# Projection sessions of three halves at block borders, and expert 0's scaling on ScalarE: a mixture of experts behind a cross attention

## The chip, the cores and the metric

The kernel runs on one core of a Trainium2 chip. The metric is the time of one execution on the device, in microseconds. A core has TensorE (in the profile PE for its matmuls and PEld for its weight loads), VectorE (DVE), ScalarE (ACT), GpSimd (POOL) and SyncE (SP), each with a queue of its own that it works through in order, and they wait for each other by semaphores. TensorE writes into PSUM, which has eight banks of 128 x 512 numbers of 32 bits; ScalarE and VectorE carry its results from there to SBUF.

## The reference

`x` is (8, 8, 512, 64): batch, head, token, channel. `state` is (8, 8, 32, 64). Both parts of the attention read each other, and the joined result goes through eight experts, all of which see every row:

```python
    a = softmax(scale * x @ state.T);   xread = a @ state
    a2 = softmax(scale * state @ x.T);  sread = a2 @ x
    attn = np.concatenate([xread, sread], axis=2)        # per batch: 512 + 32 rows
    x = attn.transpose(0, 2, 1, 3).reshape(4352, 512)
    P = sinkhorn(exp(x @ w_gate))                        # 4352 x 8, 8 rounds
    for e in range(8):
        h = np.maximum(x @ w1[e], 0.0)                   # 512 -> 1024
        out += P[:, e:e + 1] * (h @ w2[e])               # 1024 -> 512
```

## The kernel before, in words

**Stages.** Up to about 137 us the kernel computes the attention, the gate with its Sinkhorn rounds, and expert 0, in an order that a small planner (`issue`, line 48) works out from estimated costs. From there on the order is written out by hand (the loop at line 872), and the change lies in that part: experts 1 to 7.

**Blocks.** The rows are cut into nine blocks (line 122). Blocks 0 to 7 hold the 512 token rows of one batch each, block 8 the 256 state rows of all batches. The loop goes through `work`, the pairs (expert e, block bi) with e from 1 to 7: 63 pairs, of which the last has a tail of its own (`layer2_last`, line 258), so that 62 go through `layer2`.

**Projection.** `xread` is a weighted sum of 32 state vectors per head, so the kernel doesn't form it for blocks 0 to 7. It multiplies the state with `w1` first: V (line 196), which `project` (line 192) makes for one pair (e, bi). V has F = 1024 columns, made in two **halves** f of 512 columns. A half is eight matmuls on tiles of 64 x 32 of the array (line 204) into two PSUM banks `v_ps`, q = 0 and 1, and two copies by ScalarE to SBUF (line 208). What I call a **session** is one uninterrupted run of such matmuls; here it is one call of `project` with two halves, four banks. Three V tiles are there at a time (line 158).

**Layer 1.** `layer1` (line 227) is a generator. Each of its eight steps makes one **hidden tile**: two matmuls of 512 columns (line 219; four of 256 columns in block 8) into a bank `hps`, and a relu by ScalarE into `Hm` (line 239). `hps` and `v_ps` share a ring of four banks, tag "h". After the fourth and the eighth step VectorE makes four sums and differences of the hidden tiles (lines 245 to 248), which I call a group of sums.

**Layer 2.** `layer2` (line 279) multiplies with seven products instead of eight, by the sums of hidden tiles and of weights (T, lines 171 to 179). It is a generator of seven steps, each one product of eight matmuls (four in block 8; line 293) and what follows it:

```python
        product(A, h(0, 0), w2h[:, :NJ, :DH], True)
        nc.scalar.copy(out=Bb[:, :nk], in_=A[:, :nk])      # line 320
        product(Eb, s(0), T[:, 0], True);  add(Eb, 1, 1)   # E
        product(Bb, s(1), T[:, 1]);        add(Bb, 0, 1)   # B
        product(A, h(1, 0), w2h[:, NJ:, :DH]); add(A, 0, 0)
        product(Bb, h(0, 1), T[:, 2]);     add(Bb, 1, 1)   # B
        product(Eb, s(2), w2h[:, NJ:, DH:]); add(Eb, 0, 1) # E
        product(Bb, h(1, 1), T[:, 3]);     add(Bb, 1, 0)   # B
```

A and E have one PSUM bank each; B has two, the `seeds` (line 318), used in turn (line 319). The profile calls the B banks Bseed. `add` (line 303) multiplies a product by the column of P for this expert and adds it to `acc` in SBUF, one VectorE instruction per 128 rows and 256 columns (line 307). So seven products sit in four banks, and a product may only go on in its bank once the add before it has read it.

**How they are woven.** Block i's layer 2 and block i + 1's layer 1 alternate by the pattern at line 885: behind the seven products stand 0, 0, 1, 2, 2, 2 and 1 hidden tiles. Behind the first product, A, stands the session for block i + 2 (line 883). Block 6 of each expert has no session, since block i + 2 is block 8, and block 7 of expert 7 has none, since nothing is left to project. A step counter (`step`, line 862) calls the loader of the next expert's weights (`load_w`, line 160) at every sixth step: four DMAs on GpSimd's queue, and later eight differences of weights on VectorE.

**Scaling.** Expert 0's result is stored in `acc` unscaled, since P isn't known yet. In expert 1 `weigh` (line 251) multiplies each block's rows in `acc` by column 0 of P, on GpSimd, one instruction per 128 rows: blocks 0 and 1 at the start of block 0, then always one block ahead (line 310).

Of the kernel before, what the change touches and what calls it, by code (L numbers as in the profile page):

```python
# [9 lines left out]
FP32 = mybir.dt.float32  # L10
FP16 = mybir.dt.float16
AX_X = mybir.AxisListType.X
ALU = mybir.AluOpType
AF = mybir.ActivationFunctionType
EPS = 1e-9


class Ring:
# [71 lines left out]
def kernel(  # L90
# [9 lines left out]
    nc = tc.nc  # L100

    B, H, S, D = x.shape
    Ns = state.shape[2]
    Dm, E = moe_w_gate.shape
    F = moe_w1.shape[2]
# [4 lines left out]
    NTB = N // 128  # L110
    NSC = S // 128
    NP = H // 2
    NQ = NP // 2
# [8 lines left out]
    blocks = [(b * S, S) for b in range(B)] + [(NX, B * Ns)]  # L122
# [10 lines left out]
    def bank(shape, dtype, name, tag="bank"):  # L133
        return pools[tag].tile(shape, dtype, name=name, tag=tag)
# [23 lines left out]
    vpool = ctx.enter_context(tc.tile_pool(name="vpool", bufs=3))  # L158
# [24 lines left out]
    w16 = [None] * E  # L183
# [5 lines left out]
    asb = actx.enter_context(tc.tile_pool(name="attn_sb", bufs=2))  # L189
    spl = actx.enter_context(tc.tile_pool(name="stprep", bufs=1))  # L190

    def project(e, bi):
        if bi == B:
            return
        w1h = w16[e][0]
        V = vpool.tile([128, NQ, F], FP16, name="V", tag="V")
        vt[(e, bi)] = V
        for f in range(F // 512):
            cols = ds(f * 512, 512)
            ps = [bank([128, 512], FP32, "v_ps", ring[0]) for _ in range(NQ)]  # L200
            for j in range(4):
                for q in range(NQ):
                    r = ((j ^ q) % 2) * 64
                    nc.tensor.matmul(ps[q][ds(j * Ns, Ns), :], stT[ds(r, 64), bi, q, ds((j ^ q) * Ns, Ns)],  # L204
                                     w1h[ds(r, 64), 2 * q + j // 2, cols],
                                     tile_position=(r, j * Ns))
            for q in range(NQ):
                nc.scalar.copy(out=V[:, q, cols], in_=ps[q])  # L208

    def hidden_ps(e, bi, fb, out):  # L210
        w1h = w16[e][0]
# [7 lines left out]
            nc.tensor.matmul(out, lhs, rhs, start=(k == 0), stop=(k == len(terms) - 1))  # L219

    vt = {}
    ring = ["bank"]
    hid = {}
    final = (E - 1, B)
    seeds = []

    def layer1(e, bi):

        t0, tn = blocks[bi]
        th = tn // 2  # L230
        Hm = hpool.tile([128, 2, NJ, S], FP16, name="Hm", tag="Hm")
        sm = hpool.tile([128, 3, NJ, S // 2], FP16, name="sm", tag="sm")
        hid[(e, bi)] = (Hm, sm)
        for j in range(NJ):
            for i in range(2):
                fb = i * NJ + j
                hps = bank([128, S], FP32, "hps", "h")
                hidden_ps(e, bi, fb, hps[:, :tn])
                nc.scalar.activation(out=Hm[:, i, j, :tn], in_=hps[:, :tn], func=AF.Relu)  # L239
                if j % 2 and i and (e, bi) != final:  # L240
                    jj = ds(j - 1, 2)
                    a11, a21 = Hm[:, 0, jj, :th], Hm[:, 0, jj, th:tn]
                    a12, a22 = Hm[:, 1, jj, :th], Hm[:, 1, jj, th:tn]
                    s1, s2, s4 = (sm[:, k, jj, :th] for k in range(3))
                    nc.vector.tensor_add(s1, a21, a22)  # L245
                    nc.vector.tensor_sub(a21, a11, a21)  # L246
                    nc.vector.tensor_sub(s2, s1, a11)  # L247
                    nc.vector.tensor_sub(s4, a12, s2)  # L248
                yield

    def weigh(b):
        if b < len(blocks):
            t0, tn = blocks[b]
            for k in range(t0 // 128, (t0 + tn) // 128):
                nc.gpsimd.tensor_scalar(out=acc[:, k, :], in0=acc[:, k, :], scalar1=Pmat[:, k, 0:1],  # L255
                                        scalar2=None, op0=ALU.mult)

    def layer2_last():
        e, bi = final
# [19 lines left out]
    def layer2(e, bi, n):  # L279
        t0, tn = blocks[bi]  # L280
        nk = tn // 256
        th = tn // 2
        Hm, sm = hid.pop((e, bi))
        w2h, T = w16[e][1], tsum[e]
        tb = t0 // 128
        p = Pmat[:, :, e:e + 1]
        A = bank([128, 2, DH], FP32, "A", "A")
        Eb = bank([128, 2, DH], FP32, "E", "E")

        def product(dst, lhs, rhs, first=False):  # L290
            for c in range(nk):
                for j in range(NJ):
                    nc.tensor.matmul(dst[:, c], lhs(j, c), rhs[:, j],  # L293
                                     start=first and c == 0 and j == 0, stop=(j == NJ - 1),
                                     skip_group_check=True)

        def h(i, half):
            return lambda j, c: Hm[:, i, j, ds(half * th + c * 128, 128)]

        def s(k):  # L300
            return lambda j, c: sm[:, k, j, ds(c * 128, 128)]

        def add(src, row, col):
            for c in range(nk):
                k = tb + row * nk + c
                dst = acc[:, k, ds(col * DH, DH)]
                nc.vector.scalar_tensor_tensor(out=dst, in0=src[:, c], scalar=p[:, k], in1=dst,  # L307
                                               op0=ALU.mult, op1=ALU.add)

        if e == 1:  # L310
            for b in range(2) if bi == 0 else (bi + 1,):
                weigh(b)
        product(A, h(0, 0), w2h[:, :NJ, :DH], True)
        if not n:
            for i in range(2):
                bb = pb.tile([128, 2, DH], FP32, name="Bseed%d" % i)
                nc.tensor.matmul(bb.rearrange("p c d -> p (c d)"), identh, aT[:, 0, 0], start=True, stop=True)
                seeds.append(bb)
        Bb = seeds[n % 2]
        nc.scalar.copy(out=Bb[:, :nk], in_=A[:, :nk])  # L320
        yield
        product(Eb, s(0), T[:, 0], True)
        add(Eb, 1, 1)
        yield
        product(Bb, s(1), T[:, 1])
        add(Bb, 0, 1)
        yield
        product(A, h(1, 0), w2h[:, NJ:, :DH])
        add(A, 0, 0)
        yield  # L330
        product(Bb, h(0, 1), T[:, 2])
        add(Bb, 1, 1)
# [54 lines left out]
    for g in range(2):  # L387
# [10 lines left out]
        out=wg_st, in_=moe_w_gate.rearrange("(kc p) e -> p kc e", p=128)))  # L398
# [28 lines left out]
    for g in range(4):  # L427
        ps = psum([128, 4, 128], FP16, "stT_ps")
# [13 lines left out]
    def gmul(_):  # L442
        for b in range(B):
            for j in range(4):
                for q in range(NQ):
# [6 lines left out]
                  lambda eng, q=q: copy(eng, G[:, :, q], gps[q].tile), [gm_op], uses=[gps[q]])  # L452
# [201 lines left out]
    def tile_of(tag, shape):  # L654
# [15 lines left out]
        out=Pmat, in_=logits, func=AF.Exp, bias=sm_["nm"]), [c])  # L670
# [137 lines left out]
    for bi in range(2):  # L808
# [14 lines left out]
        for j in range(NJ):  # L823
# [32 lines left out]
    for tag in ("A", "E"):  # L856
        pools[tag] = ctx.enter_context(
            tc.tile_pool(name="psum_" + tag, bufs=1, space=bass.MemoryType.PSUM))
    ring[0] = "h"
    n = 0  # L860

    def step():
# [6 lines left out]
                wload.pop(0)  # L869

    work = [(e, bi) for e in range(1, E) for bi in range(len(blocks))]
    for i, (e, bi) in enumerate(work):
        if bi == 1 and e + 1 < E:
            wload.append(load_w(e + 1))
        if (e, bi) == final:
            layer2_last()
            break
        l2 = layer2(e, bi, i)
        l1 = layer1(*work[i + 1]) if i + 1 < len(work) and work[i + 1] not in hid else iter(())
        for k in range(7):  # L880
            next(l2)
            step()
            if k == 0 and i + 2 < len(work) and work[i + 2] not in vt:
                project(*work[i + 2])
            for _ in range((0, 0, 1, 2, 2, 2, 1)[k]):
                next(l1, None)
                step()
        for part in (l1, l2):
            for _ in part:
                pass  # L890
        if bi == len(blocks) - 3:
            for _ in (x for w in wload for x in w):
                pass
            wload.clear()
# [30 lines left out]
```

## Time and profile before

| | |
|---|---|
| median of 3 executions | 766.16 us (766.08 to 768.02) |
| the profiled execution | 765.04 us |
| its span, first to last instruction | 763.3 us |
| granted TensorE clock, mean | 1.00 |
| busy TensorE, VectorE, ScalarE, GpSimd | 747.2, 626.8, 513.3, 104.5 us |

All rows of the profile are of one execution. Its time is 1.7 us above its span, which is what lies around the first and the last instruction.

How to read the rows. In the timeline a row has the start in us from the span's start, the duration of the merged group, the engine, the line of the kernel, the operation, output<-inputs with their shape, and the count; in brackets stands the idle time of the engine ahead of it and what ended it. Matmuls overlap, and their ends are modelled, so the distance between two starts says more than a duration. In the groups by line stand the count, then busy us and mean ns of one, then the idle time ahead. In the list of waits stand the engine and line that waited, what it waited for, the sum in us, how often, and the longest. "issue" is idle time for which the profile shows no releaser.

### The profile page before, as it was taken

What the parts mean: (1) busy time and instruction counts of PE and PEld (TensorE: products, weight loads), DVE (VectorE), ACT (ScalarE), POOL (GpSimd) and SP (SyncE); (2) the same over time, 40 slices, a digit from 0 to 9 for tenths busy, and PEclk for the clock granted to TensorE, in tenths of its full rate; (3) what the DMA queues carried; (4) which work ended last, traced back from release to release, by engine and by line L of the source; (5) the groups of instructions that cost most, each with busy time, mean ns of one, the idle gap of its engine ahead of it and who ended that gap; (6) DMA issues with size and microseconds to landing.
All of it is one profiled execution on the core that took longest, in us unless ns stands there. A gap on an engine that the chain in (4) does not pass through costs nothing.

```text
span 763.3 us, 16286 instructions
## 1 busy us (share of the span) xinstructions
PE 747.2 (98%) x6557; PEld 501.5 (66%) x6557; DVE 626.8 (82%) x1533; ACT 513.3 (67%) x1002; POOL 104.5 (14%) x102
## 2 busy tenths in 40 slices
PE   5999999999999999999999999999999999999997
PEld 3444445566776667766776666766677666767676
DVE  6998977888987888888897888888887888878885
ACT  5888976666667675766657665676656666576652
POOL 4433100799200000100001000000001000000000
PEclk9999999999999999999999999999999999999999
DMA  8997200060015000510006000240006000002334
GB/s 135 190 147 123 46 1 1 1 112 1 1 24 89 1 2 1 88 25 2 1 1 111 2 1 1 38 75 1 1 2 101 11 2 1 1 34 85 104 111 139
DMA packets 41595, 34.61 MB, mean 45 GB/s; under 512 B 16688, under 2 KB 33072, under 8 KB 41520
## 3 DMA queue, kind: packets, MB, share of 16 engines
q0 software_dynamic: 21248, 20.97, 17.7%
q1 hardware_dynamic: 19040, 12.08, 6.0%
q8 instruction: 51, 0.84, 0.5%
q10 hardware_dynamic: 1232, 0.52, 0.3%
q14 instruction: 24, 0.20, 0.1%
HBM read 42.48 MB, written 8.91 MB: 67 GB/s over the span
## 4 chain that ended last, share of the span: by engine, by line
PE 91%; DVE 5%; ACT 3%; DMA 1%; issue 0%
PE hps L219 27%; PE Bseed L293 20%; PE E L293 14%; PE A L293 13%; PE yps L769 7%; PE v_ps L204 4%; PE hps L734 4%; DVE acc L307 1%; DVE sm L245 1%; ACT Hm L239 1%; PE su_ps L609 1%; DMA st_st<-in_state_dram 1%; ACT V L370 1%; PE y L271 0%; PE v_ps L712 0%; ACT xT L370 0%
## 5 line engine op out<-in xcount | busy, mean ns | idle before, releaser
L239 ACT ACTIVATE Hm<-hps 128x512 f16<-128x512 f32 (+1 forms) x496 | 266.1, 572 | 188.4 <-PE hps L219 173.4
L219 PE MATMUL hps<-aT,V 128*128 128x512 f16 x880 | 234.9, 379 | 0.0
L293 PEld LDWEIGHTS <-Hm 128*128 128x128 f16 x1888 | 184.6, 98 | 68.9 <-ACT Hm L376 0.3
L307 DVE SCALAR_TENSOR_TENSOR acc<-Bseed,Pmat,acc 128x256 f32<-128x256 f32 x354 | 155.4, 478 | 56.6 <-PE Bseed L293 54.1
L293 PEld LDWEIGHTS <-sm 128*128 128x128 f16 x1416 | 133.1, 98 | 51.8 <-DVE sm L245 23.8
L293 PE MATMUL A<-w2h,Hm 128*128 128x256 f16 x944 | 123.5, 273 | 0.0
L293 PE MATMUL Bseed<-T,Hm 128*128 128x256 f16 x944 | 123.3, 273 | 0.0
L219 PEld LDWEIGHTS <-V 128*128 128x128 f16 x880 | 86.1, 98 | 45.2
L208 ACT CAST V<-v_ps 128x512 f16<-128x512 f32 x216 | 111.2, 608 | 0.0
L307 DVE SCALAR_TENSOR_TENSOR acc<-E,Pmat,acc 128x256 f32<-128x256 f32 x236 | 103.3, 477 | 4.5 <-PE E L293 0.9
L245 DVE TENSOR_TENSOR sm<-Hm 128x512 f16<-128x512 f16 (+1 forms) x122 | 51.1, 419 | 19.3 <-ACT Hm L239 18.5
L769 PE MATMUL yps<-w2h,hT 128*128 128x512 f16 x272 | 66.5, 380 | 0.0
L307 DVE SCALAR_TENSOR_TENSOR acc<-A,Pmat,acc 128x256 f32<-128x256 f32 x118 | 51.9, 479 | 15.8 <-PE A L293 15.7
L293 PE MATMUL E<-T,sm 128*128 128x256 f16 x472 | 63.7, 274 | 0.6
L293 PE MATMUL Bseed<-T,sm 128*128 128x256 f16 x472 | 61.8, 273 | 0.0
L293 PE MATMUL E<-w2h,sm 128*128 128x256 f16 x472 | 61.7, 273 | 0.0
L255 POOL TENSOR_SCALAR acc<-acc,Pmat 128x512 f32<-128x512 f32 x34 | 55.2, 1638 | 44.8 <-DVE Pmat L686 44.8
L166 POOL DMA_DIRECT2D w1h<-in_moe_w_dram x12 | 8.6, 720 | 355.2 <-PE hps L219 355.2
L248 DVE TENSOR_TENSOR sm<-Hm,sm 128x512 f16<-128x512 f16 (+1 forms) x122 | 52.5, 430 | 4.2
L246 DVE TENSOR_TENSOR Hm<-Hm 128x512 f16<-128x512 f16 (+1 forms) x122 | 51.0, 418 | 4.2
L247 DVE TENSOR_TENSOR sm<-sm,Hm 128x512 f16<-128x512 f16 (+1 forms) x122 | 49.4, 405 | 0.0
L320 ACT COPY Bseed<-A 128x512 f32<-128x512 f32 (+1 forms) x62 | 34.1, 549 | 18.7 <-PE A L293 17.2
(110 smaller groups left out, 561.6 us busy)
## 6 DMA issues: line engine op xcount, KB each, us to landing
w1h<-in_moe_w_dram POOLq DMA_DIRECT2D x16, 512.0 KB, 7.1
w2h<-in_moe_w_dram POOLq DMA_DIRECT2D x16, 512.0 KB, 7.7
out_dram<-acc SPq DMA_DIRECT2D x32, 256.0 KB, 2.8
x_nat<-in_x_dram POOLq DMA_DIRECT2D x16, 256.0 KB, 5.9
st_st<-in_state_dram SPq DMA_DIRECT2D x1, 256.0 KB, 4.5
st_st<-in_state_dram ACTq DMA_DIRECT2D x1, 256.0 KB, 4.9
out_dram<-acc SPq DMA_DIRECT2D x4, 64.0 KB, 1.7
out_dram<-acc ACTq DMA_DIRECT2D x4, 64.0 KB, 2.0
```

What stands on the lines that cost most here:

```text
L208: nc.scalar.copy(out=V[:, q, cols], in_=ps[q])
L219: nc.tensor.matmul(out, lhs, rhs, start=(k == 0), stop=(k == len(terms) - 1))
L239: nc.scalar.activation(out=Hm[:, i, j, :tn], in_=hps[:, :tn], func=AF.Relu)
L245: nc.vector.tensor_add(s1, a21, a22)
L246: nc.vector.tensor_sub(a21, a11, a21)
L247: nc.vector.tensor_sub(s2, s1, a11)
L248: nc.vector.tensor_sub(s4, a12, s2)
L255: nc.gpsimd.tensor_scalar(out=acc[:, k, :], in0=acc[:, k, :], scalar1=Pmat[:, k, 0:1], scalar2=None, op0=ALU.mult)
L293: nc.tensor.matmul(dst[:, c], lhs(j, c), rhs[:, j], start=first and c == 0 and j == 0, stop=(j == NJ - 1), skip_group_check=True)
L307: nc.vector.scalar_tensor_tensor(out=dst, in0=src[:, c], scalar=p[:, k], in1=dst, op0=ALU.mult, op1=ALU.add)
L320: nc.scalar.copy(out=Bb[:, :nk], in_=A[:, :nk])
L769: nc.tensor.matmul(yps.tile, hT[fb].tile[:, ds(tk * 128, 128)], w2h[:, fb, :], start=(fb == 0), stop=(fb == NFB - 1))
```

## The change

It has four parts, and all of it concerns experts 1 to 7.

1. `project` becomes a generator over a list of halves, which need not belong to one block. The table `SESS` says at the border of which blocks a session stands and how many halves it takes: three at blocks 7, 0, 2, 3 and 5, one at block 6, none at 1, 4 and 8. The very first, ahead of expert 1's block 0, takes two. A session now stands ahead of the block's first product. Of three halves the first uses the E bank and the B bank that this block is about to use; the other two use the four banks of the ring. Its first half is copied at once, the others after the A product.
2. The patterns of hidden tiles change: `PATV` in a block with a session, `PAT0` in one without, `PATS` in block 8, `PATN` in a block 7 without a session. All end with 0: no hidden tile stands behind the last product.
3. The first group of sums of each expert's block 0, which is made during block 8 of the expert before, is emitted one step later, behind the next product's add (`late`).
4. `weigh` takes one row block of 128 at a time. The first block's four go to VectorE, ScalarE, VectorE and GpSimd; all others to ScalarE, one behind each of the last four products of the block before, while expert 1 runs.

```diff
+SESS = {7: 3, 0: 3, 2: 3, 3: 3, 5: 3, 6: 1}
+PATV = (0, 0, 1, 3, 2, 2, 0)
+PAT0 = (0, 1, 1, 2, 2, 2, 0)
+PATS = (1, 1, 1, 1, 2, 2, 0)
+PATN = (1, 1, 1, 2, 2, 1, 0)
...
-    def project(e, bi):
...
+    def project(halves, n):
+        banks = []
+        for k, (e, bi, f) in enumerate(halves, 3 - len(halves)):
+            if (e, bi) not in vt:
+                vt[(e, bi)] = vpool.tile([128, NQ, F], FP16, name="V", tag="V")
+            w1h = w16[e][0]
             cols = ds(f * 512, 512)
-            ps = [bank([128, 512], FP32, "v_ps", ring[0]) for _ in range(NQ)]
+            if k:
+                ps = [bank([128, 512], FP32, "v_ps", "h") for _ in range(NQ)]
+            else:
+                ps = [bank([128, 512], FP32, "v_ps", "E"), seeds[n % 2].rearrange("p c d -> p (c d)")]
...
-            for q in range(NQ):
-                nc.scalar.copy(out=V[:, q, cols], in_=ps[q])
+            banks.append([(vt[(e, bi)][:, q, cols], ps[q]) for q in range(NQ)])
+        for dst, src in sum(banks[:-2], []):
+            nc.scalar.copy(out=dst, in_=src)
+        yield
+        for dst, src in sum(banks[-2:], []):
+            nc.scalar.copy(out=dst, in_=src)
+        yield
...
+                    if bi == 0 and j == 1:
+                        late.append(sums)
+                    else:
+                        sums()
...
-    def weigh(b):
...
+    def weigh(k, eng):
+        if eng == "ACT":
+            nc.scalar.mul(acc[:, k, :], acc[:, k, :], Pmat[:, k, 0:1])
+        else:
+            (nc.vector if eng == "DVE" else nc.gpsimd).tensor_scalar(
+                out=acc[:, k, :], in0=acc[:, k, :], scalar1=Pmat[:, k, 0:1], scalar2=None, op0=ALU.mult)
...
-        if e == 1:
-            for b in range(2) if bi == 0 else (bi + 1,):
-                weigh(b)
+        if not n:
+            for k, eng in enumerate(("DVE", "ACT", "DVE", "POOL")):
+                weigh(k, eng)
...
+    halves = [(e, bi, f) for e, bi in work if bi < B and (e, bi) not in vt for f in range(F // 512)]
     for i, (e, bi) in enumerate(work):
...
+        v, pat = iter(()), PATS if bi == B else PATN if bi == B - 1 else PAT0
+        if bi in SESS and halves:
+            some = SESS[bi] if i else F // 512
+            v, pat = project(halves[:some], i), PATV
+            del halves[:some]
+        next(v, None)
         l2 = layer2(e, bi, i)
...
         for k in range(7):
             next(l2)
             step()
-            if k == 0 and i + 2 < len(work) and work[i + 2] not in vt:
-                project(*work[i + 2])
-            for _ in range((0, 0, 1, 2, 2, 2, 1)[k]):
+            if k == 0:
+                next(v, None)
+            if late:
+                late.pop()()
+            if e == 1 and bi < B and 3 <= k < 7:
+                m = blocks[bi + 1][0] // 128 + k - 3
+                if m < NTB:
+                    weigh(m, "ACT")
+            for _ in range(pat[k]):
                 next(l1, None)
                 step()
```

More of the change, by code (lines that the diff above doesn't have):

```diff
@@ L190 @@
     spl = actx.enter_context(tc.tile_pool(name="stprep", bufs=1))
-    def project(e, bi):
[L193 to L198, printed above, removed]
+    def project(halves, n):
[4 more added lines that the diff above has]
+            w1h = w16[e][0]
             cols = ds(f * 512, 512)
-            ps = [bank([128, 512], FP32, "v_ps", ring[0]) for _ in range(NQ)]
+            if k:
+                ps = [bank([128, 512], FP32, "v_ps", "h") for _ in range(NQ)]
+            else:
+                ps = [bank([128, 512], FP32, "v_ps", "E"), seeds[n % 2].rearrange("p c d -> p (c d)")]
             for j in range(4):
@@ L221 @@
     vt = {}
-    ring = ["bank"]
     hid = {}
+    late = []
     final = (E - 1, B)
@@ L240, in layer1, with sums @@
                 if j % 2 and i and (e, bi) != final:
[L241 to L248, printed above, removed]
-                yield
-    def weigh(b):
[L252 to L256, printed above, removed]
+                    def sums(jj=ds(j - 1, 2)):
+                        a11, a21 = Hm[:, 0, jj, :th], Hm[:, 0, jj, th:tn]
+                        a12, a22 = Hm[:, 1, jj, :th], Hm[:, 1, jj, th:tn]
+                        s1, s2, s4 = (sm[:, k, jj, :th] for k in range(3))
+                        nc.vector.tensor_add(s1, a21, a22)
+                        nc.vector.tensor_sub(a21, a11, a21)
+                        nc.vector.tensor_sub(s2, s1, a11)
+                        nc.vector.tensor_sub(s4, a12, s2)
+                    if bi == 0 and j == 1:
+                        late.append(sums)
+                    else:
+                        sums()
+                yield
+    def weigh(k, eng):
[4 more added lines that the diff above has]
+                out=acc[:, k, :], in0=acc[:, k, :], scalar1=Pmat[:, k, 0:1], scalar2=None, op0=ALU.mult)
     def layer2_last():
@@ L858 @@
             tc.tile_pool(name="psum_" + tag, bufs=1, space=bass.MemoryType.PSUM))
-    ring[0] = "h"
     n = 0
```

## The prediction

> **What bounds the kernel now.** I read the page first, engines and then the chain that ended last.
>
> ```profile
> span 763.3 us, 16286 instructions
> PE 747.2 (98%) x6557; PEld 501.5 (66%) x6557; DVE 626.8 (82%) x1533; ACT 513.3 (67%) x1002; POOL 104.5 (14%) x102
> PE 91%; DVE 5%; ACT 3%; DMA 1%; issue 0%
> ```
>
> TensorE (PE) is the path. A busy PE isn't a PE without gaps, so the next view is its timeline, late in expert 7, where blocks with and without a projection stand side by side.
>
> ```profile
> 716.53 0.63 PE L204 MATMUL v_ps<-w1h,stT 64*32 64x512 f16 x16
> 717.09 1.05 PE L293 MATMUL E<-T,sm 128*128 128x256 f16 x8
> 717.97 1.04 PE L293 MATMUL Bseed<-T,sm 128*128 128x256 f16 x8
> 718.84 0.59 PE L219 MATMUL hps<-aT,V 128*128 128x512 f16 x2
> ...
> 725.79 1.04 PE L293 MATMUL A<-w2h,Hm 128*128 128x256 f16 x8
> ...
> 736.02 1.04 PE L293 MATMUL A<-w2h,Hm 128*128 128x256 f16 x8
> 736.89 1.27 PE L293 MATMUL E<-T,sm 128*128 128x256 f16 x8
> 738.00 1.04 PE L293 MATMUL Bseed<-T,sm 128*128 128x256 f16 x8
> ...
> 745.82 1.04 PE L293 MATMUL A<-w2h,Hm 128*128 128x256 f16 x8
> ```
>
> Starts, not modelled ends, are to be read. A product of eight matmuls takes 0.87 us (717.97 to 718.84). A block with a projection lasts 10.23 us (725.79 to 736.02), one without 9.80 (736.02 to 745.82), and in the latter E takes 1.11 (736.89 to 738.00) instead of 0.87: 0.24 is a wait. So a bare block is 9.56 us, a hidden tile of two matmuls in it (9.56 - 7 x 0.87)/8 = 0.43, and a session of two halves costs 10.23 - 9.56 = 0.67.
>
> ```profile
> PEld L293 <- DVE sm L245: 23.8, 60, 0.4
> PEld L204 <- issue: 11.6, 54, 0.4
> L204 PE MATMUL v_ps<-w1h,stT 64*32 64x512 f16 x864 | 33.8, 381 | 0.0
> 164.17 0.62 PE L204 MATMUL v_ps<-w1h,stT 64*32 64x512 f16 x16
> 164.39 0.40 PE L204 MATMUL v_ps<-w1h,stT 64*32 64x512 f16 x8
> 747.13 1.10 PEld L293 LDWEIGHTS <-sm 128*128 128x128 f16 x11 [0.34 <-DVE sm L245]
> ```
>
> There are 864/16 = 54 sessions in 62 layer-2 blocks. In each, the second half's eight matmuls start 0.22 us after the first's (164.39 - 164.17). So 2 x 0.22 is streaming and 0.67 - 0.44 = **0.23 is the price of a session as such**. The row of waits gives nearly the same by itself: 11.6/54 = 0.21 us of idle weight load ahead of each. The E wait is real only without a session; where there is one, it covers the wait (E starts 0.56 after the session does, 716.53 to 717.09). That leaves 62 - 54 = 8 exposed waits. Nothing else stands in PE's way, so the change can win only in these two places.
>
> **The change, part by part.**
>
> *Sessions.* The 108 halves stay. The new table makes six sessions in each of experts 1 to 6 (15 halves in the first, then 16) and five (13 halves) in expert 7: 41, of which 33 have three halves, seven one, one two. Thirteen sessions less at 0.23: **-3.0 us** (-2.8 by the row of waits). A third half is priced like the second, 0.22: its weights load in the same stream.
>
> *The E waits.* Every pattern but the old one ends its hidden tiles before the last product, so the second group of sums starts one product earlier than now. 8 x 0.24 = **-1.9 us**.
>
> *What the new order leans on.* I lay out one three-half block from the start of its A product: E 0.87, B 1.74, hidden 2.61, A 3.04, three hidden 3.91 to 5.21, B 5.21, two hidden 6.08, E 6.95, two hidden 7.82, B 8.69, next session 9.56. The other engines' durations:
>
> ```profile
> 163.20 1.04 PE L293 MATMUL A<-w2h,Hm 128*128 128x256 f16 x8
> 164.32 0.57 ACT L320 COPY Bseed<-A 128x512 f32<-128x512 f32 x1 [0.32 <-PE A L293]
> 154.45 2.06 ACT L208 CAST V<-v_ps 128x512 f16<-128x512 f32 x4
> 201.97 1.03 PE L219 MATMUL hps<-aT,V 128*128 128x512 f16 x4
> 202.61 1.08 ACT L239 ACTIVATE Hm<-hps 128x512 f16<-128x512 f32 x2 [0.65 <-PE hps L219]
> 201.50 0.43 DVE L245 TENSOR_TENSOR sm<-Hm 128x512 f16<-128x512 f16 x1 [0.18 <-ACT Hm L239]
> 203.10 0.42 DVE L178 TENSOR_TENSOR T<-w2h 128x512 f16<-128x512 f16 x1
> 203.43 0.87 DVE L307 SCALAR_TENSOR_TENSOR acc<-E,Pmat,acc 128x256 f32<-128x256 f32 x2
> 204.22 0.87 DVE L307 SCALAR_TENSOR_TENSOR acc<-Bseed,Pmat,acc 128x256 f32<-128x256 f32 x2
> 746.65 0.42 DVE L245 TENSOR_TENSOR sm<-Hm 128x512 f16<-128x512 f16 x1 [0.18 <-ACT Hm L239]
> ```
>
> ScalarE (ACT) takes 0.49 us per copy or relu in a row ((2.06 - 1.08)/2) and 0.59 for the last; a relu starts 0.21 after its tile ends (202.61 against 201.97 + 0.43); four sums take 1.60 (201.50 to 203.10), two adds 0.79 to the next (203.43 to 204.22) and 0.87 to their end; PE follows VectorE (DVE) by 0.06 (747.13 against 746.65 + 0.42).
>
> First tight place: A is copied to B's bank from 1.12 (164.32 - 163.20) to 1.69; B wants it at 1.74, or 1.75 with that 0.06. The session used to cover this. Second: the four late V copies run from 1.61 to 3.67, relu 1 from 3.57, relu 2 from 4.55, relu 4 from 5.53 to 6.12. The first sums then hold DVE until 7.75, and only behind them stands the add of the 5.21 product, until 8.62, or 8.68 for PE; the product at 8.69 writes that bank. Both margins are nil. What else waits has room: the E add ends at 9.41 and the session takes that bank at 9.66; relu 8 ends at 9.55, its bank is wanted near 10.1; the hidden tile that takes the last copied bank starts at 4.78, 1.1 behind the copy. In the half blocks the first sums are put behind the 5.21 product's add, which keeps them out of its way; the eight sums per expert for the next weights, 0.33 each on DVE, keep their places by step count, and one ahead of an E add stays about within its 0.25 of room. For the tight places nothing shows a stall. A gain they can't give, as PE runs back to back; above I bound them by 0.1 us a block, a semaphore's 0.06 and some. I take 0.02 in 41 blocks: **+0.8** (0 to 4).
>
> *Scaling.* GpSimd's (POOL's) work now:
>
> ```profile
> 137.66 19.14 POOL L255 TENSOR_SCALAR acc<-acc,Pmat 128x512 f32<-128x512 f32 x12 [44.79 <-DVE Pmat L686]
> 145.60 0.87 DVE L307 SCALAR_TENSOR_TENSOR acc<-E,Pmat,acc 128x256 f32<-128x256 f32 x2
> L556 ACT ACTIVATE E<-psB,nsB 128x512 f16<-128x512 f32 x16 | 11.3, 704 | 0.3 <-DVE nsB L548 0.3
> L552 DVE TENSOR_TENSOR eA<-eA,mxA 128x512 f32<-128x512 f32 x16 | 11.4, 710 | 0.1
> ```
>
> POOL's work, 1.6 us a row (19.14/12), lay beside PE: rows 2 and 3 were ready near 137.66 + 4 x 1.6 = 144.1, the first add came at 145.60. Taking them away saves nothing directly. The 31 multiplications on ScalarE aren't in the trace; they lie between 0.59 us (a copy, above) and 0.70 (L556, which also takes an operand per partition). I take 0.70, the nearer in form, and in a row 0.60. In expert 1 one goes ahead of relu 2: relu 1 leaves ACT at 4.06, the multiplication at 4.66, against 4.55 without it; unoverlapped it would be 4.76, or 0.21 in each of five blocks with wide sums. ACT's whole load there is 15 x 0.49 + 4 x 0.60 = 9.8 of 10.4 us. **+0.3** (0 to 1.1). The weight DMAs behind POOL's work are issued earlier and wait for their buffers anyway.
>
> The Trainium skill speaks against this move: "ScalarE: Activation LUTs", section "Rules for kernel authors", says to multiply on VectorE, and its section "What ACT_TABLE_LOAD costs" prices such an operand at 93 ns, 706 ns in all (an estimate from its formula). The trace has 704 (L556) against 0.59 us; at 706 the sum is unchanged.
>
> *First block of expert 1.* Its session moves ahead of A and so ahead of banks still being emptied.
>
> ```profile
> 141.32 1.58 ACT L376 ACTIVATE Hm<-hps 128x512 f16<-128x512 f32 x3 [0.24 <-PE hps L734]
> 144.10 1.05 PE L293 MATMUL E<-T,sm 128*128 128x256 f16 x8
> ```
>
> The last relu ends at 142.90 (141.32 + 1.58). If its bank is among the session's four, E starts near 142.95 + 0.65 + 0.87 + 0.43 (session, A, and the two matmuls that seed B's banks) = 144.9 instead of 144.10; if not, as now. Two rows scaled on DVE (0.42 to 0.71 us each, between the sums and L552) end about when E's add is due. **+0.5** (0 to 0.9).
>
> Sum: -3.0 - 1.9 + 0.8 + 0.3 + 0.5 = **-3.3 us**. The profiled execution took 765.04 and would take 761.7 (span 760.0). It lies 1.1 below the median shown, 766.16, from which I forecast **762.9**.
>
> **Rivals.**
>
> *The sums get in the way (slower).* The second tight place, in the 35 such blocks with wide sums: an add behind four sums holds the bank of the last B product. It decides once VectorE is 0.1 us a block behind my count: 35 x 0.1 eats the gain. For it: no margin, and 82% load. Against: the rows quoted already hold what DVE takes with ACT and PE at full work beside it, and POOL's tensor work is gone. At 0.2 behind it adds 7: 769.9. Chance 0.11.
>
> *ScalarE binds.* Six copies a session, all on one engine, and in expert 1 the multiplications: when ACT enters a block half a microsecond late, relu 2 and all behind it slip; 8 blocks of expert 1 at 0.5 us are 4: 766.9. Against: 9.8 of 10.4 us. Chance 0.08. The Trainium skill has this case as a rule: "TensorEngine Tiling (Array Packing)", section "PSUM Bottleneck", says that packed matmuls leave the emptying of PSUM as the bottleneck and wants both engines on it. No row here shows it yet, with ACT at 67%.
>
> *A session has no fixed price.* If three halves cost 1.00 (1.5 x 0.67), the first term is gone: 765.9. For it: the split rests on starts within one session. Against: the 0.21 of idle ahead of every one. Chance 0.13. The change would then hardly do what it says.
>
> **How the numbers follow.** My forecast has 0.68, with its own range of 760.8 (no stalls, a start that costs nothing, and 0.5 for the scatter of the median) to 764.8 (stalls of 0.07 a block). The range, 760.8 to 767.5, takes in the second and third rival and leaves out the first and the tails. A measurement of this kernel tells about 0.3% (2.3 us) from no change: faster, below 763.9, is the forecast less its upper edge, 0.66; slower, above 768.5, is the first rival and a tail, 0.12; the rest, 0.22, is the same.
>
> **What would show it.** 41 sessions with 0.21 of idle each; three-half sessions near 0.88 us; blocks of 10.44, 10.01 and 9.56 us by halves; the E wait on L245 gone. Against me: waits of B's products on L307 or L320, hidden tiles waiting for V copies, a longer expert 1, or a gap ahead of 144 us.

## The result, and the profile after

The change made the kernel faster by about half a per cent: 762.18 us median (761.16 to 767.85, 22 runs) against 766.04 (764.77 to 768.53, 22 runs), a ratio of 0.9953 with a 95% interval of 0.9943 to 0.9964. That is 3.6 us, between 2.8 and 4.4. The forecast was 3.3 less and 762.9.

In the profile that was taken with the result, TensorE's granted clock was 0.93 over the first 100 us and expert 1 began 5.5 us later than in a second profile; so the rows below are from that second profiled execution of the same kernel, 762.35 us with a span of 760.6. Lines have moved: v_ps is L211, hps L231, the relu L251, the sums L257 to L260, the products L310, the adds L324, the copy of A L337. First the page.

```profile
span 760.6 us, 16196 instructions
PE 78%; DVE 1%; ACT 1%; issue 0%
PE hps L231 27%; PE Bseed L310 20%; PE A L310 14%; PE E L310 13%; PE v_ps L211 4%; DVE acc L324 1%; ACT Hm L251 1%; PE y L288 0%; DVE sm L257 0%; DVE sm L260 0%; DVE Hm L258 0%; DVE sm L259 0%; DVE T L183 0%; PE Bseed L211 0%; DVE acc L290
```

TensorE is still the path. The shares sum to 80% only, since the chain in this profile goes back no further than expert 1's first session, at 143.91 us. Now its timeline: late in expert 6 a session of one half, then late in expert 7 a block behind a session of three halves, the next session, and a block without one.

```profile
635.65 1.05 PE L310 MATMUL A<-w2h,Hm 128*128 128x256 f16 x8
...
645.32 0.41 PE L211 MATMUL v_ps<-w1h,stT 64*32 64x512 f16 x8
645.67 1.05 PE L310 MATMUL A<-w2h,Hm 128*128 128x256 f16 x8
...
693.28 1.05 PE L310 MATMUL A<-w2h,Hm 128*128 128x256 f16 x8
694.17 1.04 PE L310 MATMUL E<-T,sm 128*128 128x256 f16 x8
695.04 1.03 PE L310 MATMUL Bseed<-T,sm 128*128 128x256 f16 x8
...
701.99 1.04 PE L310 MATMUL Bseed<-T,Hm 128*128 128x256 f16 x8
703.18 0.61 PE L211 MATMUL v_ps<-w1h,stT 64*32 64x512 f16 x16
703.73 1.05 PE L310 MATMUL A<-w2h,Hm 128*128 128x256 f16 x8
...
713.31 1.04 PE L310 MATMUL A<-w2h,Hm 128*128 128x256 f16 x8
714.18 1.04 PE L310 MATMUL E<-T,sm 128*128 128x256 f16 x8
715.05 0.59 PE L231 MATMUL hps<-aT,V 128*128 128x512 f16 x2
```

From A to A it is 10.45 us with the three-half session in between (693.28 to 703.73) and 9.58 without one (703.73 to 713.31): the forecast had 10.44 and 9.56. With a session of one half it is 10.02 (635.65 to 645.67). So one half costs 0.44 and three cost 0.87: two more halves add 0.43, or 0.22 each, and about 0.22 is left that each session pays once. In the block without a session E takes 0.87 (714.18 to 715.05), where it took 1.11 before. The waits of the weight loads and of TensorE, in the rows that changed:

```profile
PEld L211 <- issue: 9.2, 41, 0.8
PE v_ps L211 <- ACT Hm L393: 0.8, 1, 0.8
```

There are 41 idle gaps ahead of sessions instead of 54, and the row of E waits for the sums, 23.8 us before, isn't there any more. New is one wait of TensorE, of the first session for a relu.

**Reading past the scatter.** Single executions differ by more than the effect, and the trace shows where: expert 1's last 16 hidden matmuls ahead of the loop start anywhere from 138.45 to 141.25 us in the other profiled executions, since the attention stage varies. So two distances are read in each profile: the **start**, from those 16 matmuls to the first E product of expert 1, and the **main stretch**, from that E product to the first y product of the tail.

| kernel | the 16 | first E | first y | start | main stretch |
|---|---|---|---|---|---|
| before | 138.52 | 144.10 | 755.66 | 5.58 | 611.56 |
| after, first profile | 144.99 | 151.29 | 758.45 | 6.30 | 607.16 |
| after, second profile | 139.48 | 145.78 | 752.94 | 6.30 | 607.16 |
| before, ScalarE scales | 138.81 | 144.39 | 755.77 | 5.58 | 611.38 |
| before, sums earlier | 139.53 | 145.12 | 754.69 | 5.59 | 609.57 |
| after, two halves a session | 138.45 | 144.75 | 755.42 | 6.30 | 610.67 |
| after, GpSimd scales | 141.25 | 147.55 | 756.63 | 6.30 | 609.08 |
| after, first session behind A | 138.90 | 144.48 | 751.65 | 5.58 | 607.17 |
| the same, multiplications behind relus | 139.45 | 145.03 | 752.67 | 5.58 | 607.64 |
| the same as the last but one, one multiplication on VectorE | 138.63 | 144.21 | 751.38 | 5.58 | 607.17 |
| after, one sum more | 139.19 | 145.49 | 773.80 | 6.30 | 628.31 |
| after, one sum more, elsewhere | 139.67 | 145.97 | 753.39 | 6.30 | 607.42 |

Both profiles of the changed kernel agree to a hundredth of a microsecond, with 4.40 won in the main stretch and 0.72 lost in the start: 3.68, which is what the times show. The main stretch can therefore carry verdicts that the times can't. Each of the other kernels has one profile only, and in two of these a single late copy (told with the last run) cost 0.27 and 0.28. So a difference of that size counts only where the blocks are named that make it.

### The profile page after: what moved, and what is told of

Read it like the earlier page. It is cut to its first block, busy times and chain, and to the rows that moved or that the text cites. A ratio compares the mean times of both kernels' runs of the same rounds, so it can differ in the third digit from the quotient of the medians.

```text
span 766.1 us, 16196 instructions
## 1 busy us (share of the span) xinstructions
PE 744.2 (97%) x6557; PEld 505.8 (66%) x6557; DVE 617.2 (81%) x1535; ACT 528.6 (69%) x1033; POOL 50.8 (7%) x69
## 4 chain that ended last, share of the span: by engine, by line
PE 78%; DVE 1%; ACT 1%; issue 0%
PE hps L231 27%; PE Bseed L310 20%; PE A L310 14%; PE E L310 13%; PE v_ps L211 4%; ACT Hm L251 1%; DVE acc L324 1%; PE y L288 0%; DVE sm L257 0%; DVE sm L260 0%; DVE Hm L258 0%; DVE sm L259 0%; DVE T L183 0%; PE Bseed L211 0%; DVE acc L290 0%
## 5 line engine op out<-in xcount | busy, mean ns | idle before, releaser
L251 ACT ACTIVATE Hm<-hps 128x512 f16<-128x512 f32 (+1 forms) x496 | 265.3, 577 | 127.9 <-PE hps L231 125.3
L231 PE MATMUL hps<-aT,V 128*128 128x512 f16 x880 | 230.2, 380 | 0.0
L310 PEld LDWEIGHTS <-Hm 128*128 128x128 f16 x1888 | 181.3, 98 | 71.4 <-issue 16.0
L324 DVE SCALAR_TENSOR_TENSOR acc<-Bseed,Pmat,acc 128x256 f32<-128x256 f32 x354 | 155.1, 478 | 9.2 <-PE Bseed L310 6.4
L310 PEld LDWEIGHTS <-sm 128*128 128x128 f16 x1416 | 138.3, 98 | 33.8
L310 PE MATMUL A<-w2h,Hm 128*128 128x256 f16 x944 | 123.8, 273 | 0.0
L310 PE MATMUL Bseed<-T,Hm 128*128 128x256 f16 x944 | 123.3, 273 | 0.0
L231 PEld LDWEIGHTS <-V 128*128 128x128 f16 x880 | 86.1, 98 | 51.4
L324 DVE SCALAR_TENSOR_TENSOR acc<-E,Pmat,acc 128x256 f32<-128x256 f32 x236 | 103.2, 477 | 12.2 <-PE E L310 12.2
L257 DVE TENSOR_TENSOR sm<-Hm 128x512 f16<-128x512 f16 (+1 forms) x122 | 50.2, 411 | 64.2 <-ACT Hm L251 64.0
L219 ACT CAST V<-v_ps 128x512 f16<-128x512 f32 x150 | 77.7, 611 | 0.0
L786 PE MATMUL yps<-w2h,hT 128*128 128x512 f16 x272 | 68.8, 390 | 0.0
L324 DVE SCALAR_TENSOR_TENSOR acc<-A,Pmat,acc 128x256 f32<-128x256 f32 x118 | 51.9, 479 | 17.2 <-PE A L310 16.7
L337 ACT COPY Bseed<-A 128x512 f32<-128x512 f32 (+1 forms) x62 | 34.1, 549 | 44.6 <-PE A L310 42.1
L310 PE MATMUL E<-T,sm 128*128 128x256 f16 x472 | 61.7, 273 | 0.0
L310 PE MATMUL E<-w2h,sm 128*128 128x256 f16 x472 | 61.7, 273 | 0.0
L310 PE MATMUL Bseed<-T,sm 128*128 128x256 f16 x472 | 61.6, 272 | 0.0
L260 DVE TENSOR_TENSOR sm<-Hm,sm 128x512 f16<-128x512 f16 (+1 forms) x122 | 50.2, 412 | 4.2
L786 PEld LDWEIGHTS <-hT 128*128 128x128 f16 x272 | 24.8, 101 | 27.4 <-issue 4.0
L393 ACT ACTIVATE hT<-hps 128x512 f16<-128x512 f32 (+1 forms) x69 | 36.0, 588 | 4.0 <-PE hps L751 3.5
```

What stands on the lines that cost most here:

```text
L219: nc.scalar.copy(out=dst, in_=src)
L310: nc.tensor.matmul(dst[:, c], lhs(j, c), rhs[:, j], start=first and c == 0 and j == 0, stop=(j == NJ - 1), skip_group_check=True)
L393: nc.scalar.activation(out=out, in_=in_, func=AF.Relu)
L786: nc.tensor.matmul(yps.tile, hT[fb].tile[:, ds(tk * 128, 128)], w2h[:, fb, :], start=(fb == 0), stop=(fb == NFB - 1))
```

## The experiments

My theory was that of the forecast: 13 sessions less at a fixed price, eight E waits gone, a first session that waits, and a new order with no room in two places. The rivals were that a session has no price of its own, that the scaling brings or costs something, and that idle time on VectorE or ScalarE makes the tight places harmless.

**The changed kernel again**, unedited.

> The changed kernel once more, unedited, for a profile in which the attention stage isn't stretched as in the first one, and for a time beside the other kernels of this call. From the start of the first E product of expert 1 to the first y product of the tail the first profile shows 607.2 us against 611.6 before; I expect the same again, within 0.2, and the whole at 3.5 us (3 to 4.5) below the kernel before. A rival by which part of the gain came from the attention stage expects a total gain that differs from 4.4 less the 0.7 that the first session loses.

762.88 us against 765.71, ratio 0.996 (0.9946 to 0.9975), which is 3.1 us; the main stretch is the same 607.16. The 3.68 of the two distances lies within that interval (1.9 to 4.1), so nothing in the times asks for a share of the attention stage.

**Is there a price per session?**

```diff
-SESS = {7: 3, 0: 3, 2: 3, 3: 3, 5: 3, 6: 1}
+SESS = {b: 2 for b in range(8)}
```

> The changed kernel with two halves in a session and a session in each of blocks 0 to 7: 54 sessions instead of 41, the same 108 halves, patterns and scaling as they are. My theory (a session has a price of its own, 0.23 us) expects it 13 x 0.23 = 3.0 us above the changed kernel, so 0.6 below the kernel before, with 54 idle gaps of 0.21 ahead of the sessions and blocks of 10.23. The rival (a half costs 0.33 wherever it stands) expects no difference from the changed kernel, 3.6 below the kernel before.

765.67 us, ratio to the kernel before 1.0003 (0.9986 to 1.0019); the main stretch is 3.51 longer than the changed kernel's. Its timeline, with sessions of two halves:

```profile
695.98 1.05 PE L310 MATMUL A<-w2h,Hm 128*128 128x256 f16 x8
...
705.65 0.63 PE L211 MATMUL v_ps<-w1h,stT 64*32 64x512 f16 x16
706.21 1.05 PE L310 MATMUL A<-w2h,Hm 128*128 128x256 f16 x8
...
716.44 1.05 PE L310 MATMUL A<-w2h,Hm 128*128 128x256 f16 x8
```

Blocks are 10.23 (695.98 to 706.21 to 716.44) as in the kernel before. The price is there, and the rival is gone: the same halves in 13 more sessions eat nearly the whole gain. The 0.5 beyond 13 x 0.23 is a balance of smaller things, read from the distances between A products. Behind a half block A follows A after 7.31 instead of 6.51 + 0.67, six times 0.13, since the last relu there ends only when the session has begun (at the first of these borders at 232.45, the session from 232.13). Expert 1's blocks lose 0.16 more beside the multiplications. On the other side, this version is spared the 0.43 that the changed kernel loses in block 6 of experts 2, 4 and 6 (see the weight sums below).

**Are the E waits real?** The kernel before, with the last hidden tile moved ahead of the last product in the eight blocks that precede a block without a session:

```diff
+        j = i + 3
+        bare = j >= len(work) or work[j][1] == B
+        pat = (0, 0, 1, 2, 2, 3, 0) if bare else (0, 0, 1, 2, 2, 2, 1)
...
-            for _ in range((0, 0, 1, 2, 2, 2, 1)[k]):
+            for _ in range(pat[k]):
```

> The kernel before, with the pattern 0, 0, 1, 2, 2, 3, 0 in the eight blocks that stand ahead of a block without a session, so that their last group of sums starts one product earlier; 54 sessions, GpSimd scales. My theory (eight exposed waits of E for these sums, 0.24 each) expects 1.9 us less than the kernel before and E products of 0.87 in those blocks. The rival (the wait is only moved, to the B product or the bank) expects no change, within 0.5.

764.07 us against 765.71, ratio 0.998 (0.9967 to 0.9994); the main stretch is 1.99 shorter, 8 x 0.25. Blocks without a session went from 9.82 to 9.56.

**Did the scaling bring anything?** Two runs: the new scaling in the old order, and the old scaling in the new one. The first, in the kernel before, with the change's `weigh`:

```diff
-        if e == 1:
-            for b in range(2) if bi == 0 else (bi + 1,):
-                weigh(b)
+        if not n:
+            for k, eng in enumerate(("DVE", "ACT", "DVE", "POOL")):
+                weigh(k, eng)
...
+            if e == 1 and bi < B and 3 <= k < 7:
+                m = blocks[bi + 1][0] // 128 + k - 3
+                if m < NTB:
+                    weigh(m, "ACT")
```

> The kernel before with the changed kernel's scaling alone: VectorE, ScalarE, VectorE and GpSimd for the first four rows, ScalarE behind the last four products of each block of expert 1. My theory (GpSimd's scaling lay beside TensorE and cost nothing, ScalarE has room in this order) expects no change, within 0.5 us, with groups of four sums at 1.60 us in expert 1 where they now take up to 2.1. The rival (GpSimd's traffic was part of the gain) expects 1 us less or better; a second one (ScalarE's multiplications hold up relus) expects up to 1.1 more.

765.4 against 765.71 us, ratio 1.0002 (0.9988 to 1.0015); the main stretch is 0.18 shorter, in expert 1 (89.23 us from A to A instead of 89.42).

The second run takes these lines back out of the changed kernel and puts the old ones in, all on GpSimd.

> The changed kernel with the scaling as it was: all on GpSimd, blocks 0 and 1 at the start, then one block ahead. If the new order has no room on VectorE, GpSimd's traffic beside it (a group of sums took up to 2.1 us instead of 1.6 there) stalls the B products of expert 1's blocks with sessions: I expect 0.3 to 0.5 in each of blocks 0, 2, 3 and 5, so 1 to 2 us, less the 0.3 that ScalarE's multiplications cost now: 0.7 to 1.7 above the changed kernel, and only in expert 1. The rival (the scaling doesn't matter in the new order either, as it didn't in the old) expects less than 0.3 either way.

763.57 against 766.13 us, ratio 0.9971 (0.9954 to 0.9987); the main stretch is 1.92 longer than the changed kernel's, all of it in expert 1 (90.58 us from A to A instead of 88.66). That is more than the 0.7 to 1.7 expected, and it falls on blocks 0 to 4, with or without a session of their own. VectorE beside GpSimd in that run, and in its block 2 the sums, the add behind them and the product that waits for it:

```profile
152.84 0.43 DVE L257 TENSOR_TENSOR sm<-Hm 128x512 f16<-128x512 f16 x1 [1.16 <-ACT Hm L251]
153.30 0.80 DVE L258 TENSOR_TENSOR Hm<-Hm 128x512 f16<-128x512 f16 x1
...
162.70 0.43 DVE L257 TENSOR_TENSOR sm<-Hm 128x512 f16<-128x512 f16 x1 [0.67 <-ACT Hm L251]
163.16 0.96 DVE L258 TENSOR_TENSOR Hm<-Hm 128x512 f16<-128x512 f16 x1
...
174.92 0.71 DVE L260 TENSOR_TENSOR sm<-Hm,sm 128x512 f16<-128x512 f16 x1
175.56 0.87 DVE L324 SCALAR_TENSOR_TENSOR acc<-Bseed,Pmat,acc 128x256 f32<-128x256 f32 x2
...
176.48 1.03 PE L310 MATMUL Bseed<-T,Hm 128*128 128x256 f16 x8
```

While GpSimd scales, one or two sums of a group take 0.71 to 0.96 us instead of 0.42. In block 2 the add behind them ends at 176.43 (175.56 + 0.87), and B starts 0.05 later. In the old order the old scaling cost 0.2 us; in the new, which has no room behind the sums, 1.9. So the move to ScalarE wins almost nothing by itself, and in the new order it keeps 1.9 of the 4.4 us.

**Is the room behind the sums really nil?** One more difference in the first group of sums, repeating its last:

```diff
-                    def sums(jj=ds(j - 1, 2)):
+                    def sums(jj=ds(j - 1, 2), j=j):
...
                         nc.vector.tensor_sub(s4, a12, s2)
+                        if j == 1 and 0 < bi < B:
+                            nc.vector.tensor_sub(s4, a12, s2)
```

> The changed kernel with one VectorE instruction more (0.34 us in a row) in the first group of sums of the 49 blocks 1 to 7; it repeats the group's last difference. My theory (the add behind that group ends 0.06 us before the B product wants its bank, in the 35 blocks with a session, and about 0.07 in the 14 without) expects 49 x 0.28 = 14 us more than the changed kernel, 10 above the kernel before, with blocks of 10.72 instead of 10.44. The rival (VectorE is busy 81% of the time, its idle time takes up 0.34 us a block) expects no difference.

782.82 us, ratio 1.0222 (1.0206 to 1.0238); the main stretch is 21.15 longer, 0.43 for each of the 49. Its list of waits and one such block (lines behind the sums stand two further down here):

```profile
PE Bseed L312 <- DVE acc L326: 13.6, 49, 0.4
```

```profile
579.53 0.42 DVE L260 TENSOR_TENSOR sm<-Hm,sm 128x512 f16<-128x512 f16 x1
579.99 0.43 DVE L262 TENSOR_TENSOR sm<-Hm,sm 128x512 f16<-128x512 f16 x1
580.33 0.87 DVE L326 SCALAR_TENSOR_TENSOR acc<-Bseed,Pmat,acc 128x256 f32<-128x256 f32 x2
...
579.95 1.03 PE L231 MATMUL hps<-aT,V 128*128 128x512 f16 x4
581.26 1.03 PE L312 MATMUL Bseed<-T,Hm 128*128 128x256 f16 x8 [0.28 <-DVE acc L326]
```

The add ends at 580.33 + 0.87 = 581.20 and B starts 0.06 later, 0.44 behind the hidden tiles' end (579.95 + 0.87 = 580.82). The extra instruction takes 0.46 in this place (579.53 to 579.99), not the 0.34 that I expected, and TensorE pays nearly all of it: so 21 us, not 14. The 0.28 of the waits is short of that, since it counts from the modelled end of the matmuls.

The same instruction in the same blocks, but behind the second A product's add:

```diff
         add(A, 0, 0)
+        if 0 < bi < B:
+            nc.vector.tensor_sub(sm[:, 2, :2, :th], Hm[:, 1, :2, :th], sm[:, 1, :2, :th])
         yield
```

> The changed kernel with the same extra VectorE instruction in the same 49 blocks as the run with one more sum, but behind the add of the second A product, ahead of the first group of sums, where VectorE now idles 1.16 us in a block with a session and 0.67 in one without. It repeats a difference that the block's layer 2 already has. My theory (what counts is the place, ahead of the add that holds B's bank or not) expects no difference from the changed kernel, within 0.5 us. The rival (VectorE's load as such) expects the same 21 us as at the other place.

761.92 against 765.55 us, ratio 0.9948 (0.9934 to 0.9961); the main stretch is 0.26 longer, all in one block (a late copy, see the last run). The same load costs 21 us in one place and at most 0.3 in the other, on an engine that idles a fifth of the time.

**Can the losses be had back?** First the start: only the very first session goes behind A.

```diff
-        next(v, None)
+        if i:
+            next(v, None)
         l2 = layer2(e, bi, i)
...
             if k == 0:
                 next(v, None)
+                if not i:
+                    next(v, None)
```

> The changed kernel, with the very first session (two halves, ahead of expert 1's block 0) put behind that block's A product again, where it stood before. My theory (at that place it waits 0.8 us for the last relu of expert 1's first hidden tiles to free a bank) expects the way from the last hidden tile to the first E product at 2.1 us instead of 2.8, and 0.7 us less in all. The rival (the wait only moves to the A or E product) expects no difference.

761.1 against 766.13 us, ratio 0.9938 (0.9925 to 0.995); the start is 5.58 again, the rest unchanged. In the changed kernel it looked like this:

```profile
139.48 3.63 PE L751 MATMUL hps<-aT,V 128*128 128x512 f16 x16
143.91 0.62 PE L211 MATMUL v_ps<-w1h,stT 64*32 64x512 f16 x16 [0.80 <-ACT Hm L393]
144.46 1.05 PE L310 MATMUL A<-w2h,Hm 128*128 128x256 f16 x8
145.35 0.59 PE L334 MATMUL Bseed<-aT,identh 128*128 128x512 f16 x2
145.78 1.04 PE L310 MATMUL E<-T,sm 128*128 128x256 f16 x8
```

Then, on top of it, the multiplications behind a step's hidden tiles instead of ahead of them:

```diff
+            for _ in range(pat[k]):
+                next(l1, None)
+                step()
             if e == 1 and bi < B and 3 <= k < 7:
                 m = blocks[bi + 1][0] // 128 + k - 3
                 if m < NTB:
                     weigh(m, "ACT")
-            for _ in range(pat[k]):
-                next(l1, None)
-                step()
```

> A version that might beat both: the changed kernel with the first session behind A, and ScalarE's multiplications behind the hidden tiles of a step instead of ahead of them, so that relu 2 isn't held up. My theory expects 0.7 less from the first and 0.3 less from the second, 1.0 below the changed kernel, with all of expert 1's blocks at 10.44, 10.01 or 9.58. The rival (a multiplication behind the relus delays the next session's copies or the copy of A) expects the second to bring nothing or to cost up to 0.5.

761.95 against 766.13 us, ratio 0.9955 (0.9939 to 0.997). Here the rival won: the main stretch is 0.47 longer than with the first edit alone. ScalarE at a block's border in expert 1, in this run:

```profile
172.83 1.08 ACT L251 ACTIVATE Hm<-hps 128x512 f16<-128x512 f32 x2
173.80 1.33 ACT L270 ACTIVATE acc<-acc,Pmat 128x512 f32<-128x512 f32 x2
175.02 0.58 ACT L216 CAST V<-v_ps 128x512 f16<-128x512 f32 x1
175.49 0.61 ACT L216 CAST V<-Bseed 128x512 f16<-128x512 f32 x1
176.13 0.57 ACT L337 COPY Bseed<-A 128x512 f32<-128x512 f32 x1
```

```profile
174.80 1.05 PE L310 MATMUL A<-w2h,Hm 128*128 128x256 f16 x8
175.68 1.04 PE L310 MATMUL E<-T,sm 128*128 128x256 f16 x8
176.75 0.49 PE L310 MATMUL Bseed<-T,sm 128*128 128x256 f16 x3
```

Two multiplications now stand back to back ahead of the session's copies. The copy of A starts 1.33 behind A's start (176.13 - 174.80) instead of 1.14 (694.42 - 693.28 in expert 7 of the changed kernel) and ends at 176.70; B starts at 176.75, 1.07 behind E instead of 0.87. That is the other tight place, and it gives way as the first did.

Last, with the first session behind A as above, the first of a block's four multiplications on VectorE, ahead of the sums, the other three where the change has them:

```diff
-                    weigh(m, "ACT")
+                    weigh(m, "DVE" if k == 3 else "ACT")
```

> A version that should beat both: the first session behind A, and of the four multiplications per block in expert 1 the first on VectorE, in its idle time behind the second A product's add, the other three on ScalarE where they were. My theory expects 0.7 less than the changed kernel from the first and 0.3 from the second, so 1.0, with expert 1's blocks at 10.44, 10.01 and 9.58 instead of 10.53, 10.10 and 9.67. The rival (VectorE's multiplication, 0.48 us, delays the sums) expects expert 1 to stay as it is or to get longer, 0.7 in all.

761.66 against 765.55 us, ratio 0.9951 (0.9934 to 0.9967). Expert 1's blocks are at 10.44, 9.58 and 10.01, and the expert at 89.18 us from A to A instead of 89.45 with the first edit alone, so 0.27 came back there. The times don't separate this version, the one before it and the changed kernel: their intervals overlap. By the start and the main stretch it is 0.7 faster than the changed kernel, and would be 1.0 but for one copy of A in expert 4 that started 0.28 late (408.74, after 0.65 of idle instead of 0.37) and so held up a B product. The run with the extra sum elsewhere had one like it, at 393.72. Why a copy starts late now and then stays open.

## Why the prediction was right

Step by step, with the 3.68 us that the profiles show:

| step | forecast | shown | by |
|---|---|---|---|
| 13 sessions less | -3.0 | -2.93 | what the other rows leave of the main stretch; 0.23 each |
| eight E waits gone | -1.9 | -1.99 | the kernel before with earlier sums |
| tight places | +0.8 | 0 | blocks at 10.44 and 9.58 |
| weight sums ahead of an E add | 0 | +0.43 | 0.14 in three experts |
| multiplications ahead of relu 2 | +0.3 | +0.27 | three blocks of expert 1 at +0.09 |
| GpSimd's traffic gone | 0 | -0.18 | the new scaling in the old order |
| first session | +0.5 | +0.72 | the start |

That the sum came out so near has some luck in it: the 0.8 that I took for the tight places wasn't needed there, and covers the 0.43 and the 0.2 that I was short elsewhere. Both ends of my own range were reckoned loosely: 760.8 needs the scaling to cost nothing as well, and stalls of 0.07 a block give 765.0, not 764.8.

*What bounds the kernel.* Right: everything won was TensorE's time, in what a session costs it and in its waits for the sums.

*The price of a session.* Right in mechanism and size. It had two independent supports, the distance between blocks and the row of idle gaps, and both held. The -2.93 is what the other rows leave; read by itself, expert 3 lasts 87.94 us from A to A instead of 88.64, with two sessions and one E wait less, so a session is (0.70 - 0.25)/2 = 0.22.

*The tight places.* The margins were computed as nil and are. In the block at 693.28 the add behind the first sums is this one:

```profile
701.05 0.87 DVE L324 SCALAR_TENSOR_TENSOR acc<-Bseed,Pmat,acc 128x256 f32<-128x256 f32 x2
```

It ends at 701.92, and B starts at 701.99; 0.06 of that is the hand-over. The forecast had 8.62 and 8.69 behind A, and it is 8.64 and 8.71. I took a stall of 0.02 a block for caution; there is none. That the margins matter was shown from the other side, by the extra sum and by the crowded border.

*Weight sums.* The statement that fell. I wrote that one of them ahead of an E add stays about within its room. In block 6 of experts 2, 4 and 6 the next session takes E's bank, and it doesn't quite:

```profile
302.15 0.42 DVE L183 TENSOR_TENSOR T<-w2h,T 128x512 f16<-128x512 f16 x1
302.49 0.87 DVE L324 SCALAR_TENSOR_TENSOR acc<-E,Pmat,acc 128x256 f32<-128x256 f32 x2
...
302.30 1.04 PE L310 MATMUL Bseed<-T,Hm 128*128 128x256 f16 x8
303.41 0.37 PE L211 MATMUL v_ps<-w1h,stT 64*32 64x512 f16 x1
303.63 0.63 PE L211 MATMUL v_ps<-w1h,stT 64*32 64x512 f16 x16
```

The add ends at 303.36 (302.49 + 0.87), and the session's first half, which takes E's bank, starts 0.05 later. Its second half starts 1.33 behind the last product's start (303.63 - 302.30) instead of 1.19 (703.18 - 701.99): 0.14. Room of 0.25 against an instruction of 0.34 and a hand-over of 0.06 should have been entered as a cost of 0.15.

*Scaling.* It costs about what was forecast, for the reason given, though in three blocks (2, 3 and 5) and not five, and though a multiplication takes 0.74 us, not 0.70. Expert 1's block 2, whose A starts at 164.91:

```profile
L270 ACT ACTIVATE acc<-acc,Pmat 128x512 f32<-128x512 f32 x31 | 22.8, 736 | 0.0
168.93 0.76 ACT L270 ACTIVATE acc<-acc,Pmat 128x512 f32<-128x512 f32 x1
169.54 1.61 ACT L251 ACTIVATE Hm<-hps 128x512 f16<-128x512 f32 x3
171.18 0.42 DVE L257 TENSOR_TENSOR sm<-Hm 128x512 f16<-128x512 f16 x1 [1.26 <-ACT Hm L251]
...
173.70 1.03 PE L310 MATMUL Bseed<-T,Hm 128*128 128x256 f16 x8
```

Relu 2 starts 4.63 behind A, 0.06 later than where nothing stands ahead of it (4.57 in the last version's block 2). The sums start 6.27 behind A instead of 6.18 (699.46 - 693.28 in the block of expert 7), and B 8.79 instead of 8.71.

"Taking them away saves nothing directly" was 0.2 off, as the old scaling slowed VectorE a little even there. The rule of the Trainium skill that speaks for VectorE ("ScalarE: Activation LUTs", "Rules for kernel authors") fits the durations here, 0.48 us on VectorE against 0.74. What decided was where in the queue the instruction stands, as the last two versions show.

*The first session.* The dear end of the range: the last relu's bank was among its four. It waited 0.80, part of which the old order had waited elsewhere.

*The rivals.* That VectorE gets in the way was the right thing to fear, and the margin decided as stated: GpSimd's scaling or one more instruction is enough. That ScalarE binds happened in one version only, and for its order, not for its load. The rule of the Trainium skill that I put beside that rival ("TensorEngine Tiling (Array Packing)", "PSUM Bottleneck") is worded with more care than I gave it: the copies out of PSUM may become the bottleneck.

## What to carry to other kernels

When one engine is the bound, look for the fixed price of each switch in its timeline, between starts, and count the switches: here thirteen of them were 2.9 of the 4.9 us that switches and waits gave. An engine's idle share says little about room; the room is what lies behind one instruction in its queue, and a move should be judged by what stands directly behind it. Where single executions scatter by more than the effect, read a distance between two marks in the trace rather than the time.

## What the runs showed of the hardware that I had not expected

Within a group of sums VectorE's instructions start 0.46 or 0.34 us apart (0.46 from 152.84 to 153.30 and again from 579.53 to 579.99, 0.34 from there to 580.33). The longer distance stands where an instruction reads what the one right before it wrote, or writes what that one read or wrote, the shorter where it does neither; that this is the cause isn't shown. The extra sum, which writes the same tile as the one before it, cost 0.46. And GpSimd's scaling stretches one or two instructions of a group of four sums, from 0.42 to as much as 0.96 us, and leaves the others as they are.
